# Picking a visit's TensorE work by a time budget in a fused attention and gated-FFN kernel

## The chip, the cores and the metric

The kernel runs on one NeuronCore of a Trainium2 chip. It is one program with five engines: TensorE (PE in the profile; its weight loads are PEld), VectorE (DVE), ScalarE (ACT), GpSimd (POOL) and SyncE (SP). The engines run their own instruction lists in order and meet at semaphores. The metric is the device time of one execution in microseconds.

## The reference

```python
# q, k, v: (8 batches, 8 heads, 1152, 64); w1, w2: (512, 1024); w3: (1024, 1024); w_out: (1024, 512)
q_pool = q.reshape(B, H, S // 2, 2, D).mean(axis=3)          # 576 pooled queries
scores = (q_pool @ k^T) / sqrt(D)
attn   = softmax(scores)
x      = (attn @ v), heads side by side                       # 4608 x 512
h      = ((x @ w1) * (x @ w2)) @ w3
out    = h @ w_out                                            # 4608 x 512, float32
```

The kernel leaves the row maximum out of the softmax (a check at the end of the fast path runs a general path if a row's sum is out of bounds) and multiplies w3 by w_out once, into T, so that the last two products become one.

## The kernel before

**Pairs.** Two heads make a pair; there are 32. For a pair, q's neighbours are added and k and q are cast to 16 bit (kq16, 14 chunks of 128: 9 of k, 4 of q, a tail of q with 64 rows), and transposed into kqT: for pairs 1 to 7 by TensorE (`transp_pe`, L228: fourteen transposes into a psc tile, then three VectorE copies), from pair 8 on by a DMA transpose. GpSimd does the casts (`prepare`, L529, for the pair two ahead) and issues the loads of the first eight pairs and of the weights; SyncE issues the later ones.

**Scores.** A score step s covers 512 of the columns (key chunk by pooled query) of a pair, for both heads: 2 to 4 matmuls into a psc tile of two PSUM banks (there are three psc tiles, used in turn), then one exp on ScalarE into a ring in SBUF (L296). Three steps make a visit (VS = 3), and there are 108 visits.

**AV.** An AV (`av_step`, L558) makes one tile of 128 queries of a pair: 18 small matmuls from the ring and v into the avb bank (L316), then on VectorE a reciprocal and a product, and for the first eight pairs, and every fifth tile, one more transpose of the tile before it by TensorE into the same bank and its copy to xT. Five AVs belong to a pair, and they may start in the visits after the one in which the pair's last score lies.

**Fills.** All other TensorE work is cut into groups that a queue hands out (`fill`, L489). First those of T (`t_groups`, L370): eight transposes of w3 (L379), or eight matmuls of 512 columns that make one row block of T (L388). Then, for each of nine chunks of 512 rows of x, sixteen projections (four matmuls of 512 columns, L409, eight where the rows wrap; VectorE copies the first of a pair, L434, and multiplies the second, L437) and four output groups (eight matmuls, L447, scaled and stored). A group of weight 2 is a row block of T or an output group, the others weigh 1. A fill writes the single mo bank, or, if it is called with `scored`, a psc tile.

**The order.** The loop at L579 writes the instruction lists out: per visit first the three scores, then AVs and fills picked by a running credit: two groups of weight 1 and then an AV, or AV, fill, AV, or a fill of weight 2 and an AV. In a visit with two fills of weight 1 the second one is in psc. After the last visit the remaining AVs alternate with fills, and then the rest of the fills follows with all psc tiles.

**The first pair** has its own code (L241 to L279): its loads are split, the casts of three k chunks and of q are on VectorE and run before the rest, and `first_turn` transposes what is there into the mo bank, with VectorE copying.

Of the kernel before, what the change touches and what calls it, by code (L numbers as in the profile page):

```python
# [8 lines left out]
FP32 = mybir.dt.float32  # L9
# [113 lines left out]
def kernel(  # L123
# [62 lines left out]
    def load_kq(p, k_eng, q_eng):  # L186
        b, h0 = p // HP, 2 * (p % HP)
        kst = att.tile([128, 2, NJ * D], FP32, tag="kst")
        k_eng.dma_start(out=kst, in_=k[b, h0:h0 + 2].rearrange("u (p c) d -> p u (c d)", p=128))
        qst = att.tile([128, 2, QM * 2 * D], FP32, tag="qst")  # L190
        qtl = att.tile([QT, 2, 2 * D], FP32, tag="qtl")
        q_eng.dma_start(out=qst, in_=q[b, h0:h0 + 2, 0:QM * 256].rearrange("u (p c) d -> p u (c d)", p=128))
        q_eng.dma_start(out=qtl, in_=q[b, h0:h0 + 2, QM * 256:S].rearrange("u (p t) d -> p u (t d)", t=2))
        kq[p] = (kst, qst, qtl)

    def load_v(p, eng):
        b, h0 = p // HP, 2 * (p % HP)
# [16 lines left out]
    def cast_v(p):  # L214
        va = vaugs[p % NVA]
        if p < NVA:
            nc.gpsimd.memset(va[:, :, :, D:E1], 1.0 / SCL)
        nc.gpsimd.tensor_copy(out=va[:, :, :, 0:D], in_=vs.pop(p).rearrange("p u (c d) -> p u c d", d=D))  # L218
# [22 lines left out]
    def first_loads():  # L241
        kst = att.tile([128, 2, NJ * D], FP32, tag="kst")
        kv = k[0, 0:2].rearrange("u (p c) d -> p u (c d)", p=128)
        qst = att.tile([128, 2, QM * 2 * D], FP32, tag="qst")
        qtl = att.tile([QT, 2, 2 * D], FP32, tag="qtl")
        qv = q[0, 0:2, 0:QM * 256].rearrange("u (p c) d -> p u (c d)", p=128)
        nc.scalar.dma_start(out=qst[:, 0, :], in_=qv[:, 0, :])
        nc.sync.dma_start(out=kst[:, :, 0:K0 * D], in_=kv[:, :, 0:K0 * D])
        nc.scalar.dma_start(out=qtl, in_=q[0, 0:2, QM * 256:S].rearrange("u (p t) d -> p u (t d)", t=2))
        nc.sync.dma_start(out=qst[:, 1, :], in_=qv[:, 1, :])  # L250
        nc.sync.dma_start(out=kst[:, :, K0 * D:], in_=kv[:, :, K0 * D:])
        kq[0] = (kst, qst, qtl)

    def first_casts():
        kst, qst, qtl = kq.pop(0)
        kv = kst.rearrange("p u (c d) -> p u c d", d=D)
        qv = qst.rearrange("p u (c t d) -> p u c t d", t=2, d=D)
        o = kq16s[0].rearrange("p c u d -> p u c d")
        nc.vector.tensor_copy(out=o[:, :, 0:K0], in_=kv[:, :, 0:K0])
        nc.vector.tensor_tensor(out=o[:, 0, NJ:NJ + QM], in0=qv[:, 0, :, 0], in1=qv[:, 0, :, 1], op=ALU.add)  # L260
        nc.gpsimd.tensor_tensor(out=kq16s[0][0:QT, NJ + QM], in0=qtl[:, :, 0:D], in1=qtl[:, :, D:2 * D], op=ALU.add)
        nc.vector.tensor_tensor(out=o[:, 1, NJ:NJ + QM], in0=qv[:, 1, :, 0], in1=qv[:, 1, :, 1], op=ALU.add)
        nc.gpsimd.tensor_copy(out=o[:, :, K0:NJ], in_=kv[:, :, K0:])
        kqT = att.tile([128, NB, 128], FP16, tag="kqT", bufs=3)
        pairs[0] = (*kq_views(kqT), kqT)

    def first_turn(*parts):
        kq16, kqT = kq16s[0], pairs[0][2]
        pt = ps.tile([128, 512], FP32, tag="mo", bufs=1, name="ptf").bitcast(FP16)
        o = 0  # L270
        for c0, c1 in parts:
            for c in range(c0, c1):
                nc.tensor.transpose(pt[:, o + (c - c0) * 128:o + (c - c0) * 128 + 128],
                                    kq16[:, c].rearrange("p u d -> p (u d)"), ident16)
            o += (c1 - c0) * 128
        o = 0
        for c0, c1 in parts:
            nc.vector.tensor_copy(out=kqT[:, c0:c1].rearrange("p c i -> p (c i)"), in_=pt[:, o:o + (c1 - c0) * 128])
            o += (c1 - c0) * 128  # L279


    def scores(s):
# [87 lines left out]
    def t_groups():  # L370
        w3T = {}

        def turn(ft):
            w3T[ft] = msb.tile([128, NF, 128], FP16, tag="w3T", bufs=2, name="w3T")

            def go(pt):
                ph = pt.bitcast(FP16)
                for a in range(NF):
                    nc.tensor.transpose(ph[:, a * 128:a * 128 + 128],  # L379
                                        w3c[ft // 4][:, ft % 4, a * 128:a * 128 + 128], ident16)  # L380

            return 1, go, lambda pt: nc.vector.tensor_copy(out=w3T[ft].rearrange("p a i -> p (a i)"),
                                                           in_=pt.bitcast(FP16))

        def mult(ft):
            def go(pT):
                for a in range(NF):
                    nc.tensor.matmul(pT, w3T[ft][:, a, :], wosb[:, a, :], start=(a == 0), stop=(a == NF - 1))  # L388

            return 2, go, lambda pT: nc.vector.tensor_copy(out=T16[:, ft, :], in_=pT)  # L390

        yield turn(0)
        for ft in range(NF):
            if ft + 1 < NF:
                yield turn(ft + 1)
            yield mult(ft)

    CH = 512

# [81 lines left out]
    def head():  # L481
        while queue and not ahead:
            try:
                ahead.append(next(queue[0]))
            except StopIteration:
                queue.pop(0)
        return ahead[0][0] if ahead else 0

    def fill(scored=False):  # L489
        n = head()  # L490
        if n:
            _, go, put = ahead.pop()
            pt = bank(scored) if put else None
            go(pt)
            if put:
                put(pt)
        return n
# [4 lines left out]
    def w3_load(r):  # L502
        nc.gpsimd.dma_start(out=w3c[r // 2][:, 2 * (r % 2):2 * (r % 2) + 2, :],
                            in_=moe_w3[256 * r:256 * r + 256, :].rearrange("(c p) f -> p c f", p=128))
# [12 lines left out]
    for t in kq16s:  # L517
        nc.gpsimd.memset(t[QT:128, NB - 1], 0.0)
    first_casts()
    w3_load(0)  # L520
    w_load(wosb, moe_w_out)
    cast_kq(1)
    load_kq(2, nc.gpsimd, nc.gpsimd)
    load_v(1, nc.gpsimd)
    cast_v(0)
    w3_load(1)
    load_kq(3, nc.gpsimd, nc.gpsimd)

    def prepare(p):  # L529
# [44 lines left out]

    NVIS = NS // VS
    seen = -1
    credit = 0.0
    vis = 0
    while vis < NVIS or avn[0] < NU:  # L579
        if vis == T_START:  # L580
            queue.append(t_groups())
        while ready:
            queue.append(moe_groups(ready.pop(0)))
        if vis < NVIS:
            for s in range(vis * VS, vis * VS + VS):
                pn = (s * G + G - 1) // FLAT
                if pn != seen:
                    seen = pn
                    if pn == 0:
                        first_turn((0, K0), (NJ, NB))  # L590
                    if NPE <= pn + 1 < NP:
                        transp(pn + 1)
                    if 0 < pn < NP - 2:
                        prepare(pn + 2)
                    elif pn + 2 == NP:
                        cast_v(NP - 1)
                scores(s)
            if vis == 0:
                first_turn((K0, NJ))
                prepare(2)  # L600
        elif vis > NVIS:
            tail[0] = True
        avail = NT5 * sum(1 for e in pair_end if e < vis) - avn[0]
        turn = [p for p in range(1, NPE) if (p * FLAT // G) // VS - 1 == vis]
        if vis >= NVIS:
            fill(True)
            while avn[0] < NU:
                av_step()
                fill(True)
            break  # L610
        credit = min(credit + NU / (NVIS - 5.0), float(avail)) if avail else 0.0
        two = head() == 2
        n_av = 0 if not avail else 2 if credit >= (2.6 if two else 1.6) and avail > 1 else 1
        credit -= n_av
        n_f = 2 if n_av < 2 else 1
        if n_f == 2 and not turn:
            if not two:
                fill()
            fill(not two)
            if n_av:  # L620
                av_step()
        else:
            if n_av:
                av_step()
            for p in turn:
                transp_pe(p)
            fill()
            if n_av > 1:
                av_step()
        vis += 1  # L630
    tail[0] = True
    x_turn(NU - 1)
# [59 lines left out]
```

## Time and profile before

| | us |
|---|---|
| timed runs (3): median, lowest, highest | 428.07, 425.78, 428.37 |
| profiled execution, its own time | 426.23 |
| its span, first to last instruction | 424.5 |
| busy: TensorE, ScalarE, VectorE, GpSimd | 406.2, 326.0, 201.7, 165.3 |
| exps (L296), 324 of 1.025 mean | 307.9 |
| first exp starts | 7.87 |

All times within the execution count from the first instruction. A row of the timeline gives start, duration, engine, source line, operation, output tile and inputs, shapes, and in brackets how long the engine was idle before it and what ended that. Matmuls are pipelined: the start of a group to the start of the next is what it costs, while its duration also holds the time until its last result is out. The busy share therefore hides short waits.

### The profile page before, as it was taken

What the parts mean: (1) busy time and instruction counts of PE and PEld (TensorE: products, weight loads), DVE (VectorE), ACT (ScalarE), POOL (GpSimd) and SP (SyncE); (2) the same over time, 40 slices, a digit from 0 to 9 for tenths busy, and PEclk for the clock granted to TensorE, in tenths of its full rate; (3) what the DMA queues carried; (4) which work ended last, traced back from release to release, by engine and by line L of the source; (5) the groups of instructions that cost most, each with busy time, mean ns of one, the idle gap of its engine ahead of it and who ended that gap; (6) DMA issues with size and microseconds to landing.
All of it is one profiled execution on the core that took longest, in us unless ns stands there. A gap on an engine that the chain in (4) does not pass through costs nothing.

```text
span 424.5 us, 12640 instructions
## 1 busy us (share of the span) xinstructions
PE 406.2 (96%) x5273; PEld 249.9 (59%) x5273; DVE 201.7 (48%) x592; ACT 326.0 (77%) x358; POOL 165.3 (39%) x205
## 2 busy tenths in 40 slices
PE   4879999999999999999999999999999999999994
PEld 2457666666565656665666656665678756444442
DVE  2245554666355544554455535454355537623240
ACT  3968779889999998999889998999999990223322
POOL 4789966370571526322547314342651011000000
PEclk9999999999999999999999999999999999999998
DMA  8999998988594999969999969999991412020203
GB/s 274 252 306 295 276 301 307 283 217 242 150 284 104 270 280 292 257 131 265 306 182 343 237 155 227 246 299 294 289 203 61 58 63 65 12 101 0 99 2 105
DMA packets 90960, 86.34 MB, mean 203 GB/s; under 512 B 59664, under 2 KB 64272, under 8 KB 90896
## 3 DMA queue, kind: packets, MB, share of 16 engines
q1 hardware_dynamic: 81744, 59.78, 56.7%
q0 software_dynamic: 8720, 25.10, 21.5%
q8 instruction: 42, 0.69, 0.7%
q10 hardware_dynamic: 432, 0.59, 0.5%
q14 instruction: 22, 0.18, 0.2%
HBM read 67.11 MB, written 9.44 MB: 180 GB/s over the span
## 4 chain that ended last, share of the span: by engine, by line
PE 89%; DMA 4%; POOL 2%; DVE 2%; ACT 1%; issue 1%; SPq 0%; ACTq 0%; POOLq 0%
PE avb L316 21%; PE psc L291 18%; PE mot L409 16%; PE mo L409 14%; PE mo L447 10%; PE mot L447 5%; DMA w3c<-in_moe_w_dram 3%; PE mo L388 3%; DMA kst<-in_k_dram 1%; ACT ring L296 1%; PE ptk L233 1%; DVE kqT L235 1%; PE mot L388 0%; PE mol L469 0%; PE avb L349 0%
## 5 line engine op out<-in xcount | busy, mean ns | idle before, releaser
L296 ACT ACTIVATE ring<-psc 128x1024 f16<-128x1024 f32 x324 | 307.9, 1025 | 39.9 <-PE psc L291 38.5
L316 PEld LDWEIGHTS <-ring 128*128 128x128 f16 x2880 | 105.2, 98 | 35.4 <-issue 11.5
L316 PE MATMUL avb<-vaug,ring 128*128 128x65 f16 x2880 | 114.1, 193 | 1.5 <-DVE xT L358 1.5
L291 PE MATMUL psc<-kqT 64*128 64x512 f16 (+7 forms) x1152 | 96.2, 290 | 3.2 <-ACT ring L296 1.3
L205 POOL CAST kq<-kst 128x1152 f16<-128x1152 f32 x31 | 35.7, 1151 | 74.8 <-DMA kqT<-kq 39.2
L291 PEld LDWEIGHTS <-kqT 64*128 64x128 f16 x1152 | 45.7, 95 | 29.3 <-issue 6.1
L334 DVE RECIPROCAL rzall<-avb 128x2 f32<-128x2 f32 x160 | 26.3, 164 | 45.3 <-PE avb L316 29.8
L421 POOL DMA_DIRECT2D out_dram<-osb x21 | 11.7, 555 | 87.2 <-DVE rzall L334 87.2
L409 PEld LDWEIGHTS <-w2sb 128*128 128x128 f16 x320 | 28.3, 97 | 26.8 <-issue 2.9
L409 PEld LDWEIGHTS <-w1sb 128*128 128x128 f16 x320 | 28.0, 97 | 27.1 <-issue 3.5
L447 PEld LDWEIGHTS <-gT 128*128 128x128 f16 x280 | 25.4, 98 | 31.2 <-issue 4.0
L447 PE MATMUL mo<-T,gT 128*128 128x512 f16 x184 | 43.7, 380 | 0.0
L409 PE MATMUL mot<-xT,w2sb 128*128 128x512 f16 (+2 forms) x172 | 41.1, 364 | 0.0
L209 POOL TENSOR_TENSOR kq<-qst 128x512 f16<-128x512 f32 x31 | 39.4, 1272 | 1.1 <-DMA qst<-in_q_dram 1.1
L437 DVE TENSOR_TENSOR gT<-mot,asb 128x512 f16<-128x512 f32 x40 | 27.6, 691 | 23.6 <-PE mot L409 23.6
L218 POOL CAST vaug<-vst 128x1152 f16<-128x1152 f32 x32 | 36.6, 1144 | 5.0 <-DMA vst<-in_v_dram 4.1
L409 PE MATMUL mot<-xT,w1sb 128*128 128x512 f16 (+2 forms) x152 | 38.0, 373 | 0.0
L432 ACT COPY asb<-mot 128x512 f32<-128x512 f32 x20 | 11.7, 587 | 32.7 <-PE mot L409 32.7
L434 DVE COPY asb<-mo 128x512 f32<-128x512 f32 x35 | 24.2, 691 | 25.4 <-PE mo L409 25.4
L409 PE MATMUL mo<-xT,w1sb 128*128 128x512 f16 (+2 forms) x168 | 36.1, 344 | 0.0
L460 DVE TENSOR_SCALAR osb<-mo 128x512 f32<-128x512 f32 x23 | 15.9, 692 | 42.3 <-PE mo L447 42.3
L409 PE MATMUL mo<-xT,w2sb 128*128 128x512 f16 (+2 forms) x148 | 33.0, 351 | 0.0
(67 smaller groups left out, 269.6 us busy)
## 6 DMA issues: line engine op xcount, KB each, us to landing
vst<-in_v_dram SPq DMA_DIRECT2D x25, 576.0 KB, 5.0
kst<-in_k_dram SPq DMA_DIRECT2D x23, 576.0 KB, 5.7
qst<-in_q_dram SPq DMA_DIRECT2D x23, 512.0 KB, 7.2
out_dram<-osb POOLq DMA_DIRECT2D x21, 256.0 KB, 6.1
kst<-in_k_dram POOLq DMA_DIRECT2D x8, 576.0 KB, 10.1
qst<-in_q_dram POOLq DMA_DIRECT2D x8, 512.0 KB, 10.9
vst<-in_v_dram POOLq DMA_DIRECT2D x7, 576.0 KB, 6.9
out_dram<-osb SPq DMA_DIRECT2D x10, 256.0 KB, 2.2
```

Source lines behind the costliest of these rows:

```text
L205: nc.gpsimd.tensor_copy(out=kq16[:, 0:NJ].rearrange("p c u d -> p u c d"), in_=kst.rearrange("p u (c d) -> p u c d", d=D))
L209: eng.tensor_tensor(out=kq16[:, NJ:NJ + QM].rearrange("p c u d -> p u c d"), in0=qv[:, :, :, 0], in1=qv[:, :, :, 1], op=ALU.add)
L218: nc.gpsimd.tensor_copy(out=va[:, :, :, 0:D], in_=vs.pop(p).rearrange("p u (c d) -> p u c d", d=D))
L291: nc.tensor.matmul(psc[:, u, f - s * G:f - s * G + ln], kT2[u * 64:u * 64 + 64, jt, :], qpT[u * 64:u * 64 + 64, i0:i0 + ln], start=True, s ...
L296: nc.scalar.activation(out=ring[:, :, r0:r0 + G], in_=psc, func=AF.Exp, bias=0.0, scale=SCALE)
L316: nc.tensor.matmul(avb[:, o + u * E1:o + u * E1 + E1], ring[:, u, c0:c0 + 128], va[:, u, jt, :], start=(jt == 0 and u == 0), stop=(jt == N ...
L334: nc.vector.reciprocal(out=rzall[:, i, :], in_=av[:, :, D:E1].rearrange("p u o -> p (u o)"))
L409: nc.tensor.matmul(pw[:, d0:d0 + n], wt[:, mc, ft * 128:ft * 128 + 128], xT[:, mc, a:a + n], start=(mc == 0 and d0 == 0), stop=(mc == NC - ...
L434: nc.vector.tensor_copy(out=asb, in_=pa)
L437: nc.vector.tensor_tensor(out=gT[:, ft, :], in0=pb, in1=asb, op=ALU.mult)
L447: nc.tensor.matmul(po, gT[:, ft, tt:tt + 128], T16[:, ft, :], start=(ft == 0), stop=(ft == NF - 1))
L460: nc.vector.tensor_scalar_mul(out=osb, in0=po, scalar1=1.0 / (SCL * SCL))
```

## The change

The change has four parts.

- A visit's work is picked by a budget: 2.35 is added per visit, an AV takes 0.62, a unit of fill weight 0.87, a pair's transposes on TensorE 0.75; work is taken while more than 0.3 is left, and the transposes now come first. Two AVs are never next to each other within the stage while there is a fill, unless many wait.
- T is made two row blocks at a time: two groups of w3 transposes (weight 0.5 each, always both), then four groups of eight 256-column matmuls (weight 1).
- The first pair's transposes go to two PSUM banks at once and its tail to a third place: three k chunks to mo, four q chunks to avb, the tail of q to mo again after the first score. ScalarE copies the k chunks and half of the q chunks, VectorE the other half and the tail. GpSimd casts the three k chunks. The loads of q's second half and of its tail change queues.
- On GpSimd's queue the second w3 load moves ahead of the cast of v for pair 0 and the load of v for pair 1.

```diff
 def first_loads():
-        nc.scalar.dma_start(out=qtl, ...)
-        nc.sync.dma_start(out=qst[:, 1, :], in_=qv[:, 1, :])
+        nc.scalar.dma_start(out=qst[:, 1, :], in_=qv[:, 1, :])
+        nc.sync.dma_start(out=qtl, ...)
 def first_casts():
-        nc.vector.tensor_copy(out=o[:, :, 0:K0], in_=kv[:, :, 0:K0])
-        nc.vector.tensor_tensor(out=o[:, 0, NJ:NJ + QM], ...)
+        nc.gpsimd.tensor_copy(out=o[:, :, 0:K0], in_=kv[:, :, 0:K0])
+        for u in range(2):
+            nc.vector.tensor_tensor(out=o[:, u, NJ:NJ + QM], ...)
         nc.gpsimd.tensor_tensor(out=kq16s[0][0:QT, NJ + QM], ...)
-        nc.vector.tensor_tensor(out=o[:, 1, NJ:NJ + QM], ...)
-        nc.gpsimd.tensor_copy(out=o[:, :, K0:NJ], in_=kv[:, :, K0:])
+    def rest_casts():
+        nc.gpsimd.tensor_copy(..., in_=kv[:, :, K0:])
-    def first_turn(*parts):
+    def first_turn(c0, c1, pt, *engs):
+        for c in range(c0, c1):
+            nc.tensor.transpose(pt[:, (c - c0) * 128:(c - c0) * 128 + 128], ...)
+        w = (c1 - c0) // len(engs)
+        for n, eng in enumerate(engs):
+            o = n * w
+            eng(out=kqT[:, c0 + o:c0 + o + w]..., in_=pt[:, o * 128:(o + w) * 128])
...
-            return 1, go, lambda pt: nc.vector.tensor_copy(out=w3T[ft]...)
+            return 0.5, go, lambda pt: nc.vector.tensor_copy(out=w3T[ft]...)
-        def mult(ft):
+        def mult(ft, n0):
             def go(pT):
                 for a in range(NF):
-                    nc.tensor.matmul(pT, w3T[ft][:, a, :], wosb[:, a, :], ...)
-            return 2, go, lambda pT: nc.vector.tensor_copy(out=T16[:, ft, :], in_=pT)
+                    nc.tensor.matmul(pT[:, 0:256], w3T[ft][:, a, :], wosb[:, a, n0:n0 + 256], ...)
+            return 1, go, lambda pT: nc.vector.tensor_copy(out=T16[:, ft, n0:n0 + 256], in_=pT[:, 0:256])
-        yield turn(0)
-        for ft in range(NF):
-            if ft + 1 < NF:
-                yield turn(ft + 1)
-            yield mult(ft)
+        for ft in range(0, NF, 2):
+            yield turn(ft)
+            yield turn(ft + 1)
+            for n in range(4):
+                yield mult(ft + n // 2, n % 2 * 256)
...
     load_kq(2, nc.gpsimd, nc.gpsimd)
+    w3_load(1)
+    cast_v(0)
     load_v(1, nc.gpsimd)
-    cast_v(0)
-    w3_load(1)
...
-                        first_turn((0, K0), (NJ, NB))
+                        first_turn(0, K0, turn_bank(), nc.scalar.copy)
+                        first_turn(NJ, NJ + QM, avb.bitcast(FP16), nc.vector.tensor_copy, nc.scalar.copy)
                 scores(s)
+                if s == 0:
+                    first_turn(NB - 1, NB, turn_bank(), nc.vector.tensor_copy)
...
-        credit = min(credit + NU / (NVIS - 5.0), float(avail)) if avail else 0.0
-        two = head() == 2
-        n_av = 0 if not avail else 2 if credit >= (2.6 if two else 1.6) and avail > 1 else 1
...
+        budget += 2.35
+        for p in turn:
+            transp_pe(p)
+            budget -= 0.75
+        n_av = n_f = 0
+        if avail > 3:
+            was_av = False
+        while True:
+            late = avail > 3 and n_av < 2
+            if avail and (budget > 0.3 or late) and not (was_av and head()):
+                av_step()
+                avail -= 1
+                n_av += 1
+                budget -= 0.62
+                was_av = True
+            elif head() and budget > 0.3:
+                two_turns = head() < 1
+                budget -= 0.87 * fill(n_f == 1)
+                n_f += 1
+                if two_turns and head() < 1:
+                    budget -= 0.87 * fill(n_f == 1)
+                    n_f += 1
+                was_av = False
+            else:
+                budget = min(budget, 0.0)
+                break
```

More of the change, by code (lines that the diff above doesn't have):

```diff
@@ L248, in first_loads @@
         nc.sync.dma_start(out=kst[:, :, 0:K0 * D], in_=kv[:, :, 0:K0 * D])
-        nc.scalar.dma_start(out=qtl, in_=q[0, 0:2, QM * 256:S].rearrange("u (p t) d -> p u (t d)", t=2))
-        nc.sync.dma_start(out=qst[:, 1, :], in_=qv[:, 1, :])
+        nc.scalar.dma_start(out=qst[:, 1, :], in_=qv[:, 1, :])
+        nc.sync.dma_start(out=qtl, in_=q[0, 0:2, QM * 256:S].rearrange("u (p t) d -> p u (t d)", t=2))
         nc.sync.dma_start(out=kst[:, :, K0 * D:], in_=kv[:, :, K0 * D:])
@@ L254, in first_casts @@
     def first_casts():
-        kst, qst, qtl = kq.pop(0)
+        kst, qst, qtl = kq[0]
         kv = kst.rearrange("p u (c d) -> p u c d", d=D)
@@ L258, in first_casts, with turn_bank @@
         o = kq16s[0].rearrange("p c u d -> p u c d")
-        nc.vector.tensor_copy(out=o[:, :, 0:K0], in_=kv[:, :, 0:K0])
-        nc.vector.tensor_tensor(out=o[:, 0, NJ:NJ + QM], in0=qv[:, 0, :, 0], in1=qv[:, 0, :, 1], op=ALU.add)
+        nc.gpsimd.tensor_copy(out=o[:, :, 0:K0], in_=kv[:, :, 0:K0])
+        for u in range(2):
+            nc.vector.tensor_tensor(out=o[:, u, NJ:NJ + QM], in0=qv[:, u, :, 0], in1=qv[:, u, :, 1], op=ALU.add)
         nc.gpsimd.tensor_tensor(out=kq16s[0][0:QT, NJ + QM], in0=qtl[:, :, 0:D], in1=qtl[:, :, D:2 * D], op=ALU.add)
-        nc.vector.tensor_tensor(out=o[:, 1, NJ:NJ + QM], in0=qv[:, 1, :, 0], in1=qv[:, 1, :, 1], op=ALU.add)
-        nc.gpsimd.tensor_copy(out=o[:, :, K0:NJ], in_=kv[:, :, K0:])
         kqT = att.tile([128, NB, 128], FP16, tag="kqT", bufs=3)
         pairs[0] = (*kq_views(kqT), kqT)
-    def first_turn(*parts):
+    def rest_casts():
+        kv = kq.pop(0)[0].rearrange("p u (c d) -> p u c d", d=D)
+        nc.gpsimd.tensor_copy(out=kq16s[0].rearrange("p c u d -> p u c d")[:, :, K0:NJ], in_=kv[:, :, K0:])
+    def first_turn(c0, c1, pt, *engs):
         kq16, kqT = kq16s[0], pairs[0][2]
[L269 to L279, printed above, removed]
+        for c in range(c0, c1):
+            nc.tensor.transpose(pt[:, (c - c0) * 128:(c - c0) * 128 + 128],
+                                kq16[:, c].rearrange("p u d -> p (u d)"), ident16)
+        w = (c1 - c0) // len(engs)
+        for n, eng in enumerate(engs):
+            o = n * w
+            eng(out=kqT[:, c0 + o:c0 + o + w].rearrange("p c i -> p (c i)"), in_=pt[:, o * 128:(o + w) * 128])
+    def turn_bank():
+        return ps.tile([128, 512], FP32, tag="mo", bufs=1, name="ptf").bitcast(FP16)
     def scores(s):
@@ L380, in go @@
                                         w3c[ft // 4][:, ft % 4, a * 128:a * 128 + 128], ident16)
-            return 1, go, lambda pt: nc.vector.tensor_copy(out=w3T[ft].rearrange("p a i -> p (a i)"),
+            return 0.5, go, lambda pt: nc.vector.tensor_copy(out=w3T[ft].rearrange("p a i -> p (a i)"),
                                                            in_=pt.bitcast(FP16))
-        def mult(ft):
+        def mult(ft, n0):
             def go(pT):
                 for a in range(NF):
-                    nc.tensor.matmul(pT, w3T[ft][:, a, :], wosb[:, a, :], start=(a == 0), stop=(a == NF - 1))
-            return 2, go, lambda pT: nc.vector.tensor_copy(out=T16[:, ft, :], in_=pT)
-        yield turn(0)
-        for ft in range(NF):
-            if ft + 1 < NF:
-                yield turn(ft + 1)
-            yield mult(ft)
+                    nc.tensor.matmul(pT[:, 0:256], w3T[ft][:, a, :], wosb[:, a, n0:n0 + 256],
+                                     start=(a == 0), stop=(a == NF - 1))
+            return 1, go, lambda pT: nc.vector.tensor_copy(out=T16[:, ft, n0:n0 + 256], in_=pT[:, 0:256])
[4 more added lines that the diff above has]
+                yield mult(ft + n // 2, n % 2 * 256)
     CH = 512
@@ L519 @@
     first_casts()
+    rest_casts()
     w3_load(0)
@@ L576 @@
     seen = -1
-    credit = 0.0
+    budget = -0.6
+    was_av = False
     vis = 0
@@ L597 @@
                 scores(s)
+                if s == 0:
+                    first_turn(NB - 1, NB, turn_bank(), nc.vector.tensor_copy)
             if vis == 0:
-                first_turn((K0, NJ))
+                first_turn(K0, NJ, turn_bank(), nc.vector.tensor_copy)
                 prepare(2)
@@ L610 @@
             break
-        credit = min(credit + NU / (NVIS - 5.0), float(avail)) if avail else 0.0
-        two = head() == 2
-        n_av = 0 if not avail else 2 if credit >= (2.6 if two else 1.6) and avail > 1 else 1
[L614 to L620, printed above, removed]
-                av_step()
[L622 to L629, printed above, removed]
+        budget += 2.35
[8 more added lines that the diff above has]
+            if avail and (budget > 0.3 or late) and not (was_av and head()):
+                av_step()
+                avail -= 1
[9 more added lines that the diff above has]
+                    n_f += 1
+                was_av = False
+            else:
+                budget = min(budget, 0.0)
+                break
         vis += 1
```

## The prediction

> **What bounds the kernel now.** I read the page first: engine shares, slices, chain.
>
> ```profile
> PE 406.2 (96%) x5273; PEld 249.9 (59%) x5273; DVE 201.7 (48%) x592; ACT 326.0 (77%) x358; POOL 165.3 (39%) x205
> ...
> PE 89%; DMA 4%; POOL 2%; DVE 2%; ACT 1%; issue 1%; SPq 0%; ACTq 0%; POOLq 0%
> ```
>
> TensorE is busy 96% of the span and is 89% of the chain that ended last. An average over stages says little, so the busy sums by stretch come next (span 424.5 us, cut at 29, 75 and 345 us).
>
> ```profile
> core 0: us, PE busy (x) PEld busy (x) DVE busy (x) ACT busy (x) POOL busy (x), PEclk, DMA share, GB/s
> 0.00:29.00 29.00, 18.64 (x196) 11.35 (x198) 8.35 (x21) 18.28 (x19) 19.95 (x34) 1.00 1.01 275
> 29.00:75.00 46.00, 44.12 (x689) 29.73 (x689) 24.05 (x87) 39.10 (x42) 36.56 (x49) 1.00 1.01 297
> 75.00:345.00 270.00, 269.56 (x3896) 172.15 (x3896) 138.32 (x417) 246.06 (x259) 106.04 (x119) 1.00 0.92 223
> 345.00:424.50 79.50, 73.91 (x503) 36.63 (x497) 31.02 (x70) 22.58 (x39) 2.73 (x5) 0.98 0.18 58
> ```
>
> From 75 us on TensorE never stops (269.56 of 270), while ScalarE is idle 24 us. All TensorE work is fixed in amount, so from there a new order can only add stalls or remove what is hardly there. Something can be won in the first 29 us (10.4 us idle) and in 29:75 (1.9 us idle, and some more hidden in stretched matmuls).
>
> Then the timeline, for what a stall looks like. Columns: start, duration, engine, line, operation; the bracket is idle time and who ended it.
>
> ```profile
> 17.99 0.95 PE L379 MATMUL mo<-ident,w3c 128*128 128x128 f16 x8
> ...
> 18.78 0.61 PE L379 MATMUL mot<-ident,w3c 128*128 128x128 f16 x8
> ...
> 19.32 0.74 PE L291 MATMUL psc<-kqT 64*128 64x192 f16 x8
> ...
> 19.58 0.68 DVE L382 COPY w3T<-mot 128x1024 f16<-128x1024 f16 x1
> ...
> 20.32 0.39 PE L291 MATMUL psc<-kqT 64*128 64x320 f16 x4 [0.26 <-DVE w3T L382]
> ```
>
> This is visit 3, the only visit of the scores' stage (108 in all) that ends in a fill that borrowed a psc bank. There are three psc tiles, used in turn: three scores, then the fill takes the first again, so the next visit's **third** score is the one that must wait until VectorE has emptied the fill's. It started 1.00 us after its visit (20.32 − 19.32); in an undisturbed visit the third score starts at 0.447 (median from 75 us on, by the starts of single matmuls).
>
> ```profile
> 127.34 0.94 PE L291 MATMUL psc<-kqT 64*128 64x512 f16 x10
> ...
> 129.09 1.03 PE L409 MATMUL mot<-xT,w1sb 128*128 128x512 f16 x4
> ...
> 129.95 0.71 PE L316 MATMUL avb<-vaug,ring 128*128 128x65 f16 x18
> ...
> 130.15 0.69 DVE L434 COPY asb<-mot 128x512 f32<-128x512 f32 x1 [0.17 <-PE mot L409]
> ...
> 130.59 0.61 PE L291 MATMUL psc<-kqT 64*128 64x192 f16 x8
> ```
>
> Here the same borrowing costs nothing: an AV of 0.6 us follows the fill, and VectorE is done at 130.84, before the third score at 130.59 + 0.447 = 131.04. So the tile is free 0.89 us after the fill's successor begins, plus 0.05 (20.27 to 20.32) for the signal.
>
> **The change, part by part.**
>
> *The picks (visits 4 to 107).* Following the loop's arithmetic: 2.35 a visit, 0.62 for an AV, 0.87 for a unit of fill. Two AVs and a projection (2.11) leave 0.24, below 0.3; a projection, an AV and a projection (2.36) are the other usual visit. As two AVs may not touch, the second kind is always fill, AV, fill, and the last fill is in psc (its number is 1). 23 visits end that way (20, 23, 26, 29, 36, ... 106); before, this order was fill, fill, AV. The scores now follow the fill directly. Price of one: the fill's last matmul starts 0.216 before an AV could; the tile is free 0.216 + 0.89 + 0.05 = 1.16 after that matmul; without the wait the third score would come at 0.216 + 0.447 = 0.66. That is **0.50 lost**, in it about 0.09 for scores behind 512-column matmuls (T at 61.41 to the scores at 63.23: 1.82, elsewhere 1.73). 23 × 0.50 = 11.5 us. Ends: 0.35 (no such 0.09, VectorE 0.06 earlier) and 0.60 (the 0.55 of visit 3 and some queue on VectorE), 8.1 to 13.8. The AV behind the third score, and all after it, waits in TensorE's one order; ScalarE, with its 24 us idle, is not held up.
>
> The other boundaries: 16 more visits end in a fill in mo, 16 × 0.09 = 1.4, against 38 fewer scores behind an AV at 0.05 (AV before scores 0.607, before a fill 0.554), 1.9: near zero together, counted as zero. 15 more visits begin with an AV, where the scores' block takes 0.785 instead of 0.758: 0.4.
>
> *Transposes of q and k on TensorE (pairs 2 to 7) move to the front of their visit*, right behind the scores. They take a psc tile too, that of the visit's first score, and so wait for its exp:
>
> ```profile
> 14.44 1.65 PE L233 MATMUL ptk<-ident,kq 128*128 128x128 f16 x14 [0.31 <-ACT ring L296]
> ...
> 66.51 0.83 PE L291 MATMUL psc<-kqT 64*128 64x384 f16 x10
> ...
> 67.00 2.85 ACT L296 ACTIVATE ring<-psc 128x1024 f16<-128x1024 f32 x3 [0.42 <-PE psc L291]
> ...
> 68.77 0.71 PE L316 MATMUL avb<-vaug,ring 128*128 128x65 f16 x18 [0.72 <-DVE xT L358]
> ```
>
> The first line is pair 1, which stood so already. Later an exp begins 0.49 after its scores and takes 1.02: free at 1.51, 1.57 with the signal, against 0.77 when the scores are issued. 0.80 for each of pairs 3 to 7 (pair 2 is in the opening below) is 4.0 us; ends 0.31 (the row shown) and 0.85: 1.5 to 4.3. Before, an AV stood between, and at 50.68 the fourteen took 0.78 with no wait.
>
> *Removed.* The last line above: AV 19 directly behind AV 18 waits for VectorE; its boundary costs 0.93 where 0.05 is usual. That was the only such pair before. Three lone w3 transposes between AVs (33.54, 45.91, 57.34) took 0.88, 0.81, 0.88 instead of 0.45; T waited twice 0.17 for its copy (42.72, 53.53), pair transposes twice 0.18, a third score once 0.32 (58.91). Together 0.88 + 1.23 + 0.34 + 0.36 + 0.32 = 3.1 us, all gone if the new order has none of its own; ends 1.5 and 3.6.
>
> *T in halves.* Sixteen groups of eight 256-column matmuls (16 such take 1.76 us at L469, so 0.88 each), 14.1 us, for eight of 1.73, 13.8: 0.2 us. VectorE's copies of half size are hidden, but two halves in a row in visit 3 share mo.
>
> *The opening.* q's second half lands at 4.91 and its add ends at 5.35, as before. But four transposes (5.41 on) no longer wait for q's tail (6.09), and VectorE and ScalarE copy side by side: scores at about 6.5 instead of 7.22, first exp at 7.15 instead of 7.87. GpSimd's cast of k (0.36 on VectorE, some 0.5 by its 0.82 for twice the size) ends near 4.6, long before. The tail's add ends at 6.0, its transposition stands behind score 0, its copy is there at 7.5, and score 1 is in time for the exp at 8.15. ScalarE then runs without a break to visit 3, 0.7 early.
>
> Visit 3 takes T0 into its own: w3 transposes to 18.6, then T0 waits for wosb, which landed at 20.11 and whose place in GpSimd's queue is the same. First half 20.15 to 21.05, copied by 21.65; second half to 22.6, as it reuses mo. Scores of visit 4 at 22.6 (19.32 before), AV 0, half of T1, AV 1, scores of visit 5 at 25.55 to 26.35 (a tile waits for an exp at 26.0), pair 2 at 27.05 (its exp; GpSimd's casts end at 25.06), half of T1, AV 2, scores of visit 6 at 29.4. Before, that point was 28.96, but with one w3 transposition (0.45) more and T1 (1.73) less done: 0.8 us won. The second w3 load, now ahead of v's, lands some 2 us earlier than 27.76, so the 1.73 us wait for it goes; late next are the exp and mo. v of pair 1 lands 2 us later, and behind its cast stand on GpSimd the loads for pairs 2 and 4, and pair 3's casts, done near 35 and needed near 39. Ends: 2.0 won (wosb earlier) and 1.7 lost.
>
> Until 18.7 TensorE issued a w3 transpose every 0.108 us, then every 0.056 (the lines at 17.99 and 18.78: 0.95 and 0.61); the record of the granted clock begins there. Should it go on at the slower pace through T0 and the scores of visit 4, that is 2 × 0.88 + 0.76 = 2.5 us more; I count on the same turning point, as what it has to do before 18.7 is the same.
>
> The Trainium skill, "TensorE: Matmul & The Clock Gate", Part 1, says that TensorE runs at half rate until some 3.4 us of sustained work and falls back after such an idle window. The pace at 17.99 agrees; that the new wait for wosb would trip it, no row shows. By that rule the sum could be 441.
>
> **Sum.** 11.5 + 4.0 + 0.4 + 0.2 − 3.1 − 0.8 = +12.2. The profiled execution took 426.23 (span 424.5): 438.4. The three timed runs have 425.78 to 428.37, median 428.07, 1.8 above it; I say **438.5**. Ends added up: 8.1 + 1.5 + 0.6 − 3.6 − 2.0 = +4.6 and 13.8 + 4.3 + 0.6 − 1.5 + 1.7 = +18.9, so 431 to 445.
>
> **The rivals.**
>
> *Faster, at 420.* The opening gives all that its rows lose (0.7 of the start, 1.73 for w3, 0.56 of pair 2's wait at 25.12, 0.5 of visit 4's scores: 3.5), 29:75 its 3.1, and psc never binds: 426.2 − 6.6 + 0.6. For it: TensorE's 10.4 idle us. Against it: the tile that visit 3 waited for. It decides at 6.0 us of psc waits: with 4.0 for pairs 3 to 7, at 0.09 for each of the 23 visits. Chance 0.10.
>
> *The picks change little, 427.* The sum of work is the same, and at 127.34 (third score 0.10 late, waiting for the exp that held its tile) ScalarE's pace already costs a visit what a full tile would. Then 23 × 0.10 + 1.5 − 3.9 + 0.6 = +0.5. Against it: VectorE's copy alone takes 0.69. Chance 0.10.
>
> *Above 443.* The slower pace goes on (2.5 us), and the dear ends of the fills' and the transposes' terms come with it: 438.4 + 2.5 + 2.3 + 0.3 = 443.5. Chance 0.07.
>
> *The forecast,* 431 to 443, as the dear ends will not all come together: 0.73.
>
> A change of 1% (4.3 us) is about what timing can tell from none. Faster 0.10, same 0.10, slower 0.80. The range takes in the upper half of the second rival too (0.07 with what lies up to 431): 427 to 443.
>
> **What would show it.** Right: third scores that wait for VectorE's gT or asb copies, in 23 visits, blocks of scores of 1.25 to 1.3 us there; pairs 2 to 7 waiting for ring; TensorE's idle share up to some 6%; first exp near 7.2. Wrong: scores' blocks of 0.85 behind a fill, or scores that reach visit 6 before 28 us with T1 done.

## The result, and the profile after

The changed kernel is slower. Six runs lie between 436.62 and 441.1 us with a median of 437.33; the kernel before has 426.0 (424.73 to 428.37). The ratio is 1.0284, with a 95% interval of 1.0255 to 1.0314. The profiled execution took 440.21 us and spans 438.3.

The page of the changed kernel, engine shares and chain by engine:

```profile
PE 412.3 (94%) x5337; PEld 253.0 (58%) x5337; DVE 202.5 (46%) x596; ACT 328.4 (75%) x363; POOL 165.6 (38%) x206
...
PE 81%; DMA 6%; ACT 6%; DVE 4%; issue 2%; POOL 0%; SPq 0%; ACTq 0%; DVEq 0%
```

TensorE fell from 89% to 81% of the chain; ScalarE (1% before) and VectorE (2%) now hold 6% and 4% of it: somewhere TensorE waits for them in turn. The busy sums by stretch, with the columns as in the prediction (the stretch, its length, then PE, PEld, DVE, ACT and POOL busy, TensorE's granted clock, DMA share, GB/s), say where:

```profile
0.00:29.00 29.00, 20.21 (x165) 12.61 (x167) 6.48 (x17) 16.49 (x18) 18.11 (x32) 1.00 0.99 275
29.00:75.00 46.00, 42.83 (x751) 34.39 (x746) 25.95 (x94) 39.28 (x42) 38.76 (x51) 1.00 0.99 283
75.00:345.00 270.00, 261.69 (x3759) 159.31 (x3755) 133.19 (x404) 240.11 (x254) 106.03 (x119) 1.00 0.92 224
345.00:438.30 93.30, 87.61 (x675) 46.67 (x672) 36.87 (x83) 32.52 (x51) 2.73 (x5) 0.99 0.16 51
```

From 75 to 345 us TensorE did 269.56 us before; now 261.69, and 137 matmuls fewer. The waits of the changed kernel (who waited, for whom: us in all, times, longest) name three kinds:

```profile
PE ptk L233 <- ACT ring L298: 4.6, 7, 0.7
...
PE psc L293 <- DVE gT L440: 3.7, 16, 0.2
...
PE psc L293 <- DVE asb L437: 1.6, 7, 0.2
```

16 and 7 are 23: the 23 visits that end in a fill in a psc tile. Each is counted as 0.2 us only, because a matmul's modelled end runs into the wait; the timeline from start to start gives the whole price. One such place:

```profile
81.45 1.02 PE L412 MATMUL mot<-xT,w2sb 128*128 128x512 f16 x4
...
82.41 0.61 PE L293 MATMUL psc<-kqT 64*128 64x512 f16 x6
82.52 0.69 DVE L440 TENSOR_TENSOR gT<-mot,asb 128x512 f16<-128x512 f32 x1 [0.23 <-PE mot L412]
82.91 1.94 ACT L298 ACTIVATE ring<-psc 128x1024 f16<-128x1024 f32 x2 [0.34 <-PE psc L293]
83.26 0.39 PE L293 MATMUL psc<-kqT 64*128 64x128 f16 x4 [0.24 <-DVE gT L440]
83.59 0.72 PE L318 MATMUL avb<-vaug,ring 128*128 128x65 f16 x18
```

VectorE empties the fill's tile from 82.52 to 83.21, and the third score starts at 83.26. The scores' block is 1.18 us long (82.41 to 83.59); behind a fill in mo it is 0.76. All 23 blocks are 1.17 or 1.18.

The transpositions behind the scores:

```profile
75.31 0.83 PE L293 MATMUL psc<-kqT 64*128 64x192 f16 x12
...
76.88 0.94 PE L233 MATMUL ptk<-ident,kq 128*128 128x128 f16 x14 [0.74 <-ACT ring L298]
```

From the scores to them it is 1.57 us, where 0.76 is enough: 0.81 lost, in each of five visits.

### The profile page after: what moved, and what is told of

Same layout as the page of the kernel before. It is cut to its first block, busy times and chain, and to the rows that moved or that the text cites. A ratio compares the mean times of both kernels' runs of the same rounds, so it can differ in the third digit from the quotient of the medians.

```text
span 438.3 us, 12771 instructions
## 1 busy us (share of the span) xinstructions
PE 412.3 (94%) x5337; PEld 253.0 (58%) x5337; DVE 202.5 (46%) x596; ACT 328.4 (75%) x363; POOL 165.6 (38%) x206
## 4 chain that ended last, share of the span: by engine, by line
PE 81%; DMA 6%; ACT 6%; DVE 4%; issue 2%; POOL 0%; SPq 0%; ACTq 0%; DVEq 0%
PE avb L318 20%; PE psc L293 15%; PE mot L412 14%; PE mo L412 13%; PE mo L450 7%; PE mot L450 6%; ACT ring L298 5%; PE mo L390 3%; DMA wosb<-in_moe_w_out_dram 3%; DVE gT L440 3%; DMA xT<-xb 2%; PE ptk L233 1%; DMA kst<-in_k_dram 1%; DVE asb L437 1%; PE mol L472 0%
## 5 line engine op out<-in xcount | busy, mean ns | idle before, releaser
L318 PEld LDWEIGHTS <-ring 128*128 128x128 f16 x2880 | 103.9, 98 | 32.2 <-issue 11.4
L293 PE MATMUL psc<-kqT 64*128 64x512 f16 (+7 forms) x1152 | 100.6, 292 | 9.8 <-DVE gT L440 3.7
L412 PE MATMUL mot<-xT,w2sb 128*128 128x512 f16 (+2 forms) x180 | 42.1, 360 | 0.0
L412 PE MATMUL mo<-xT,w1sb 128*128 128x512 f16 (+1 forms) x192 | 41.3, 344 | 0.0
L437 DVE COPY asb<-mo 128x512 f32<-128x512 f32 x40 | 27.7, 692 | 28.6 <-PE mo L412 28.6
L435 ACT COPY asb<-mot 128x512 f32<-128x512 f32 x23 | 13.5, 585 | 36.2 <-PE mot L412 36.2
L450 PE MATMUL mo<-T,gT 128*128 128x512 f16 x160 | 37.8, 379 | 0.0
L412 PE MATMUL mot<-xT,w1sb 128*128 128x512 f16 x128 | 32.8, 379 | 0.0
L412 PE MATMUL mo<-xT,w2sb 128*128 128x512 f16 (+2 forms) x140 | 31.9, 355 | 0.0
L344 DVE TENSOR_TENSOR xb<-avb,rzall 128x128 f16<-128x128 f32 x96 | 28.0, 292 | 3.5 <-DMA xT<-xb 0.3
```

What stands on the lines that cost most here:

```text
L293: nc.tensor.matmul(psc[:, u, f - s * G:f - s * G + ln], kT2[u * 64:u * 64 + 64, jt, :], qpT[u * 64:u * 64 + 64, i0:i0 + ln], start=True, s ...
L318: nc.tensor.matmul(avb[:, o + u * E1:o + u * E1 + E1], ring[:, u, c0:c0 + 128], va[:, u, jt, :], start=(jt == 0 and u == 0), stop=(jt == N ...
L344: nc.vector.tensor_tensor(out=xbt, in0=av[:, :, 0:D], in1=rzall[:, i, :].unsqueeze(2).to_broadcast([128, 2, D]), op=ALU.mult)
L412: nc.tensor.matmul(pw[:, d0:d0 + n], wt[:, mc, ft * 128:ft * 128 + 128], xT[:, mc, a:a + n], start=(mc == 0 and d0 == 0), stop=(mc == NC - ...
L437: nc.vector.tensor_copy(out=asb, in_=pa)
L450: nc.tensor.matmul(po, gT[:, ft, tt:tt + 128], T16[:, ft, :], start=(ft == 0), stop=(ft == NF - 1))
```

## The experiments

Theory A says that the loss is psc tiles that are wanted before they are empty: a visit's last fill makes the next third score wait for VectorE, and leading transpositions wait for an exp. Theory B says that the budget makes visits uneven, so that ScalarE's pace of three exps (2.85 us) sets the time of some.

The experiments ran on three chips, with medians of 426.22, 426.03 and 425.86 for the kernel before, so a difference between kernels that ran on different chips holds to some tenths.

**The transpositions moved behind the first group of their visit.**

```diff
-        budget += 2.35
-        for p in turn:
-            transp_pe(p)
-            budget -= 0.75
+        budget += 2.35 - 0.75 * len(turn)
...
         while True:
+            if n_av + n_f:
+                while turn:
+                    transp_pe(turn.pop(0))
...
+        while turn:
+            transp_pe(turn.pop(0))
```

> The changed kernel with one thing altered: the six q and k transpositions on TensorE (pairs 2 to 7) come after the first group picked in their visit instead of straight behind the scores; the picks stay the same. Theory A (a transposition behind the scores waits for the exp that holds its psc tile, 0.81 us each): about 6 x 0.75 = 4.5 us less than the changed kernel, 433, and scores' blocks of 0.76 to 0.79 in those visits. Theory B (the loss comes from uneven visits that the budget makes, and ScalarE's pace): no difference, 437. Scores behind psc fills stay at 1.18.

Measured: 434.65 us (434.03 to 435.29), 1.0194 of the kernel before (1.0166 to 1.0222). That is 2.7 under the changed kernel where 4.5 was expected. That is against Theory B; Theory A has the direction, and the trace shows what it left out:

```profile
82.22 0.94 PE L233 MATMUL ptk<-ident,kq 128*128 128x128 f16 x14
...
83.00 0.71 PE L318 MATMUL avb<-vaug,ring 128*128 128x65 f16 x18
83.20 1.22 DVE L235 COPY kqT<-ptk 128x768 f16<-128x768 f16 x3
83.55 0.22 PE L351 MATMUL avb<-ident,xbt 128*128 128x128 f16 x1
83.70 1.17 PE L293 MATMUL psc<-kqT 64*128 64x384 f16 x10
```

The wait for ring is gone, but the transpositions hold a psc tile too, and its three copies end at 84.42: the third score, due at 83.70 + 0.447 = 84.15, is 0.3 late. The five scores' blocks that follow transpositions and an AV are 1.10 to 1.12 us long from start to start instead of 0.78: some 0.32 each, 1.6 us of the 1.8 that are missing. The kernel before had another fill in between.

**The order fill, fill, AV instead of fill, AV, fill.**

```diff
             if avail and (budget > 0.3 or late) and not (was_av and head()):
+                both = n_f == 1 and n_av == 0 and head() == 1 and budget - 0.62 > 0.3 and avail <= 4
+                if both:
+                    budget -= 0.87 * fill(True)
+                    n_f += 1
                 av_step()
...
-                was_av = True
+                was_av = not both
```

> The changed kernel with 21 of its 23 visits of the order fill, AV, fill turned to fill, fill, AV; the same groups in every visit. Theory A (the third score of the next visit waits until VectorE has emptied the last fill's psc tile, 0.49 us each, against 0.08 for scores behind an AV): 21 x 0.42 = 8.8 us less than the changed kernel, about 428.5, and blocks of 0.76 to 0.90 where 1.18 stood. Theory B (uneven visits, ScalarE's pace): the visits hold the same work, so 437.

Measured: 429.62 us (429.46 to 430.02), 1.008 (1.0054 to 1.0106): 7.7 less than the changed kernel, for 21 visits with the same work in each. Theory B is out for these 21. A visit's end in the repaired kernel:

```profile
78.63 0.59 PE L412 MATMUL mot<-xT,w2sb 128*128 128x512 f16 x2
...
79.06 0.71 PE L318 MATMUL avb<-vaug,ring 128*128 128x65 f16 x18
79.26 0.69 DVE L440 TENSOR_TENSOR gT<-mot,asb 128x512 f16<-128x512 f32 x1 [0.17 <-PE mot L412]
...
79.76 0.83 PE L293 MATMUL psc<-kqT 64*128 64x512 f16 x10
```

VectorE's 0.69 us now lies beside the AV. The waits of the scores for gT are no longer in the list, and of the seven for asb two are left (0.4 us), with the two blocks of 1.18 behind the two visits that were not turned.

**Both repairs.** The two diffs above, together.

> Both of these alterations of the changed kernel together. Theory A: the savings add up, 13.3 us, to 424, a little below the kernel before (426). Theory B: 437. If the two waits cover each other (a late third score hides the late transposition), clearly less than the sum, 428 or more.

Measured: 427.01 us (12 runs, 426.33 to 427.7) beside 426.22; ratio 1.0014 (0.9998 to 1.0030). The savings of the two alone, 2.7 and 7.7, add up to the 10.3 found. So undoing the two orders takes the loss away: the rest of the change (T, opening, budget) makes no difference in sum that these runs can tell. That is a balance. The blocks behind the transpositions still lose 1.7 us here and the two of 1.18 another 0.8, and the w3 load with the grouping of T wins 2.5, under the picks of the kernel before, by a run below.

**The same order put into the kernel before.**

```diff
...
             if not two:
                 fill()
+            if n_av and not two and head() == 1:
+                av_step()
+                n_av = 0
             fill(not two)
             if n_av:
                 av_step()
```

> The kernel before, with one thing altered: in its 29 visits with two fills of weight 1 and an AV, the AV stands between the fills instead of behind them; nothing else of the change. Theory A: 29 x 0.42 = 12 us more than the kernel before, 438, with scores' blocks of 1.18. Theory B: the visits hold the same work, so 426.

Measured: 435.82 us (435.59 to 437.27), 1.0231 (1.0202 to 1.0261): 9.6 us lost by this edit alone, for 29 visits.

```profile
98.74 1.02 PE L409 MATMUL mot<-xT,w1sb 128*128 128x512 f16 x4
...
99.70 0.61 PE L291 MATMUL psc<-kqT 64*128 64x512 f16 x6
99.80 0.69 DVE L434 COPY asb<-mot 128x512 f32<-128x512 f32 x1 [0.24 <-PE mot L409]
...
100.54 0.40 PE L291 MATMUL psc<-kqT 64*128 64x128 f16 x4 [0.24 <-DVE asb L434]
100.87 0.72 PE L316 MATMUL avb<-vaug,ring 128*128 128x65 f16 x18
```

The picture is the same, and all 29 blocks are 1.17 or 1.18 long. That it is 0.33 a visit and not 0.42 fits what the kernel before showed at 127.34: there third scores were often 0.1 late already, for an exp, and much of that lateness is now inside the longer wait. Added up from visit 6 on, what the other blocks last beyond 0.77 each falls from 4.0 us in the kernel before to 2.4 here.

**VectorE empties the second fill's tile twice.**

```diff
...
             if put:
                 put(pt)
+                if twice and scored:
+                    put(pt)
...
-                budget -= 0.87 * fill(n_f == 1)
+                budget -= 0.87 * fill(n_f == 1, True)
...
```

> The changed kernel, in which VectorE empties the psc tile of a visit's second fill twice (the same copy or product once more, 0.69 us each); VectorE is busy 46% of the span. Theory A (VectorE's copy is what the third score waits for): 23 visits x 0.69 = 16 us more, some 453, scores' blocks of 1.87 there. If the 0.42 comes from something else (weights that load late behind a fill, an exp): VectorE has room, 437.

Measured: 454.74 us (454.71 to 455.65), 16.9 above the changed kernel beside it (437.79). The 23 blocks grew from 1.18 to 1.89: 0.72 each, 16.5 in all.

```profile
91.70 0.61 PE L293 MATMUL psc<-kqT 64*128 64x512 f16 x6
91.81 1.42 DVE L440 TENSOR_TENSOR gT<-mot,asb 128x512 f16<-128x512 f32 x2 [0.24 <-PE mot L412]
92.20 2.86 ACT L298 ACTIVATE ring<-psc 128x1024 f16<-128x1024 f32 x3 [0.34 <-PE psc L293]
93.27 0.40 PE L293 MATMUL psc<-kqT 64*128 64x128 f16 x4 [0.96 <-ACT ring L298]
```

An engine that is busy 46% of the span passes 0.69 us of extra work on in full at these places. The bracket names ScalarE here, though the pair of products ends at 93.23 and sets the start: the exp that began at 92.20 (1.02) ends 0.01 before it. In the changed kernel the third score of the same kind of visit started at 83.26, with the exp that began at 82.91 still running, so it does not wait for that exp. The times have to be read, not the name.

**The changed kernel once more.** The same code, so there is no diff.

> The changed kernel once more, beside the others on one chip: 437. In the profiled execution of it TensorE went to its full rate at 27.1 us only and the time was 440.2; in the others, where w3's transposes, T and the first scores of visit 4 take the full rate from about 20 us, some 3 us less is expected. Theory: whether it is 437 or 440 hangs on where that turn falls, not on the order of the work.

Measured: 437.79 us (437.71 to 437.88). In this profile the record of the full TensorE clock begins at 21.6 us and the span is 435.8; in the first one it begins at 27.1 and the span is 438.3. The rows of the first:

```profile
18.24 1.03 PE L381 MATMUL mo<-ident,w3c 128*128 128x128 f16 x8
...
19.06 1.06 PE L381 MATMUL mot<-ident,w3c 128*128 128x128 f16 x8
...
20.47 1.86 PE L390 MATMUL mo<-wosb,w3T 128*128 128x256 f16 x8 [0.34 <-DMA wosb<-in_moe_w_out_dram]
...
22.85 1.86 PE L390 MATMUL mo<-wosb,w3T 128*128 128x256 f16 x8 [0.52 <-DVE T L393]
```

And the two halves of T0 in the second:

```profile
20.58 1.54 PE L390 MATMUL mo<-wosb,w3T 128*128 128x256 f16 x8
...
22.64 1.03 PE L390 MATMUL mo<-wosb,w3T 128*128 128x256 f16 x8 [0.52 <-DVE T L393]
```

From visit 3 to visit 6 it took 16.2 us (16.27 to 32.51), against 13.6 (16.80 to 30.36) in the second profile. What decides where the turn falls was not tried and stays open: the two traces have the same code and the same order.

**The opening alone, in the kernel before.** `first_loads`, `first_casts`, `rest_casts`, `first_turn` and their calls as in the change's diff; nothing else.

> The kernel before with the first pair's part of the change alone (two banks at once, its tail after the first score, ScalarE's copies, GpSimd's cast of k, the two loads exchanged); picks, T and the w3 load as before. The prediction's opening step: first exp 0.7 us earlier and kept, 425.5. What the changed kernel's trace suggests instead: the first exp 0.4 earlier, but the tail's transposition and copy stand between the first two scores and the rest of k lands 0.35 later, so that the fourth exp is no earlier: 426.2, no difference.

Measured: 427.21 us (425.49 to 429.12, 12 runs) beside 426.03; ratio 1.002 (0.9996 to 1.0044). No difference, as the second reading expected and the prediction did not.

```profile
6.48 0.29 DVE L278 COPY kqT<-avb 128x256 f16<-128x256 f16 x1 [0.70 <-PE avb L273]
...
6.80 0.37 ACT L278 COPY kqT<-avb 128x256 f16<-128x256 f16 x1 [0.83 <-DVE kqT L278]
...
7.88 3.08 ACT L298 ACTIVATE ring<-psc 128x1024 f16<-128x1024 f32 x3 [0.70 <-PE psc L293]
...
8.38 1.04 PE L293 MATMUL psc<-kqT 64*128 64x64 f16 x8 [0.32 <-DVE kqT L278]
...
11.31 1.94 ACT L298 ACTIVATE ring<-psc 128x1024 f16<-128x1024 f32 x2 [0.35 <-PE psc L293]
```

ScalarE's half of the copy does not run beside VectorE's; it waits for it. Both read the avb bank; that this is the reason was not tried. Score 1 waits for the tail's copy, so that the second exp starts 1.15 after the first, where the kernel before had 0.92, and the rest of k is transposed later, so that the fourth exp waits 0.35 more. It comes 3.43 after the first; before it was 2.73 (7.87 to 10.60).

The start of the first exp differs between executions of one opening by half a microsecond, so a single pair of profiles misleads. Over all profiles it is at 7.43 to 7.95 with the new opening (seven) and at 7.87 to 8.40 with the old one (five), and the fourth exp at 10.87 to 11.39 and at 10.60 to 11.13. By the means the new opening is 0.36 earlier at the first exp and 0.35 later at the fourth.

**A mix.** The kernel with both repairs, with the opening of the kernel before, and with AV, transpositions, fill, AV in the visits of pairs 2 to 7 where the next fill has weight 1, which is five of the six:

```diff
...
+        if turn and avail > 1 and head() == 1:
+            av_step()
+            transp_pe(turn.pop(0))
+            fill()
+            av_step()
+            budget -= 0.62 * 2 + 0.87
+            avail -= 2
+            n_av, n_f = 2, 1
+            was_av = True
...
```

> The kernel with both repairs (fill, fill, AV; transpositions not behind the scores), and further with the opening of the kernel before, and with the order AV, transpositions, fill, AV in the visits of pairs 2 to 7; T by pairs, the early w3 load and the budget stay. Theory A: the last stall of the repaired kernel, 0.3 us for the third score behind transpositions in five visits, goes: 425.5, level with the kernel before. If the new opening had been worth something, 427 or more.

Measured: 431.87 us (431.18 to 433.11), 1.0137 (1.0106 to 1.0168): a miss, 6 us above what was expected. The four picks overdraw the budget (2.86 taken of 2.35), and this shifts all picks after them. Ten visits now end in psc again, four of these with an output group of 1.73; others are left with one projection:

```profile
118.24 1.04 PE L410 MATMUL mo<-xT,w1sb 128*128 128x512 f16 x4
119.21 0.39 PE L291 MATMUL psc<-kqT 64*128 64x512 f16 x2
119.96 0.39 PE L291 MATMUL psc<-kqT 64*128 64x64 f16 x4 [0.36 <-ACT ring L296]
120.88 0.40 PE L291 MATMUL psc<-kqT 64*128 64x128 f16 x4 [0.52 <-ACT ring L296]
```

A visit of 1.5 us (117.71 to 119.21) is far shorter than its three exps, and TensorE waits for ScalarE: 2.0 us for a scores' block. This is Theory B's mechanism. It exists, and where visits are this light it costs more than a late tile. The blocks tell where most of the 4.9 us against the repaired kernel lie. From visit 6 on, beyond 0.77 each, those behind psc fills are 3.9 us longer in all, 1.8 are saved behind the transpositions, and the other blocks are 2.3 longer.

**The second w3 load alone.** In the kernel before, the load moved as in the change's last lines on GpSimd's queue.

> The kernel before with the second w3 load moved ahead of the cast of v for pair 0 and the load of v for pair 1, nothing else. The prediction's step: the wait of 1.73 us for w3 at 26 us goes, and what is late next is pair 2's transposition (ready at 25.1): 424.5, TensorE's third w3 transposition at 26.1 instead of 27.8. Rival: the wait only moves, as v of pair 1 is cast later and the loads behind it are issued later: 426.

Measured: 424.45 us (423.64 to 425.67, 12 runs) beside 425.86; ratio 0.9963 (0.9945 to 0.9980). The step counts, and what is late next is close behind:

```profile
25.23 0.95 PE L233 MATMUL ptk<-ident,kq 128*128 128x128 f16 x14
...
26.78 0.62 PE L379 MATMUL mo<-ident,w3c 128*128 128x128 f16 x8 [0.60 <-DMA w3c<-in_moe_w_dram]
...
28.26 1.15 POOL L218 CAST vaug<-vst 128x1152 f16<-128x1152 f32 x1 [2.97 <-DMA vst<-in_v_dram]
```

The wait for w3 is 0.60 instead of 1.73. The cast of v for pair 1 is indeed later (25.47 before), and nobody waited for it.

**T by pairs and in halves, with that load.** In the kernel before, `t_groups` as in the change (weight 1 for each turn) and the load moved; credit, picks and opening as before.

> The kernel before with T by pairs of w3 transpositions and halves of 256 columns, and with the same move of the w3 load; the picks, by credit, and the opening stay those of the kernel before. Prediction's steps: besides the w3 wait, the waits behind lone w3 transpositions (three of four go, 0.9), the adjacent AVs (0.9) and T's waits for its copy (0.3) go, and the halves cost 0.2: 422.5. Against it: two visits of two w3 transpositions and an AV (2.3 us of work) are shorter than three exps (2.85), 0.5 each: 423.5. If nothing of it counts: 426.

Measured: 423.37 us (422.45 to 426.01, 11 runs) beside 425.86; ratio 0.9938 (0.9919 to 0.9958). This is the best kernel found, under 1% faster than the kernel before. 2.5 us are won, 1.4 of them by the load alone, and the value lies by the expectation that counts the light visits (423.5). Those two are in the trace; behind each, the scores' block is 1.26 long, as in this one (33.37 to 34.63):

```profile
33.37 0.39 PE L291 MATMUL psc<-kqT 64*128 64x384 f16 x4
...
34.09 0.61 PE L291 MATMUL psc<-kqT 64*128 64x448 f16 x6 [0.32 <-ACT ring L296]
...
34.63 0.72 PE L316 MATMUL avb<-vaug,ring 128*128 128x65 f16 x18
```

## Why the prediction was right, point by point

The sum said +12.2 on a profiled execution of 426.23; the profiled pair differs by 14.0, and the medians by 11.3. Its terms:

- **Third scores behind a psc fill, 23 × 0.50 = 11.5.** The mechanism is shown, the net size is smaller. There are 23 waits in the list; the block is 1.18 instead of 0.785 behind an AV, and 0.095 goes to the boundary behind a fill, 0.49 together. (The prediction's sign of blocks of 1.25 to 1.3 had that boundary in the block a second time.) Undoing it gave 7.7 for 21, adding it cost 9.6 for 29, doubling VectorE's part cost 16.9. In the net it is 0.33 to 0.37 a visit, some 8 us for 23, because the AV in front of the scores has a boundary of its own and the old order already paid some lateness to the exps. The prediction weighed the first against the fills in mo and left the second out. It took the AV's boundary as 0.05; the starts give 0.08 to 0.09 (an AV takes 0.644 before scores, 0.560 before a projection).
- **Transpositions, 5 × 0.80 = 4.0.** Shown: 0.81 in each of the five visits. It is not what one gets back by moving them one place, since they hold their tile for 1.22 us of copies.
- **Removed in the stage of T, −3.1.** Right, and a little too large. Start to start, the adjacent AVs (0.88), the waits in front of pair transpositions (0.69, in four places where the prediction counted two) and those behind lone w3 transpositions (1.23, of which 0.65 stay) fell by 2.2; the waits of T for its copy (0.34) and the one late third score (0.32) are gone too, 2.8 in all. By the runs, T by pairs won 1.1 under the old picks, which have two light visits with it.
- **The opening, −0.8.** This gain did not come. Its first step, "VectorE and ScalarE copy side by side", failed: ScalarE waited for VectorE (6.36 after 6.03 in the changed kernel), and the first exp came at 7.43, not 7.15. Its second, "ScalarE then runs without a break", failed too: the fourth exp came at 10.87, where before it was 10.60. Alone, the opening is worth nothing that the runs can tell.
- **Visits 3 to 6.** The w3 wait went, as forecast (1.4 us by its own run). T0 waited for mo in both profiles (0.52), for wosb only in the first (0.34). Scores of visits 4, 5 and 6 were forecast at 22.6, 25.55 and 29.4; the second profile has 23.61, 26.50 and 30.36, all about a microsecond late. Its T0 began at 20.58 where 20.15 was forecast, and the first half of it, partly before the turn, took 0.5 longer than the second (1.54 and 1.03). In the first profile the slower pace went on to 27.1 us, the case that the prediction priced at 2.5 and held unlikely; visits 3 to 6 took 2.7 longer than in the second. That the prediction's "same turning point" does not hold is shown by the records: they begin at 18.7 in the kernel before, at 27.1 and 21.6 in the changed one, at 19.9 to 21.6 in the others.

Taken together in the profiled pair: up to visit 6 the changed kernel is at 32.51 against 28.96, with 1.28 us more work done, so 2.3 lost where 0.8 was to be won. After it, 405.8 us against 395.5 and the 1.28 less to do: 11.6 lost where 13.0 were forecast. In the second profile, whose time (437.83) is near the median, it is 0.1 and 11.2. Each time the two errors, 3.1 and 1.4 or 0.9 and 1.8, have opposite signs. The mechanism was right, but that the sum is closer than its parts is luck.

The Trainium skill, "TensorE: Matmul & The Clock Gate", Part 1, has the array at half rate until it has been busy long enough. The trace agrees in the two paces: a transposition every 0.107 us before the turn and every 0.056 after it. It does not account for when the turn comes here: by the Trainium skill some 3.4 us of sustained work are enough, while in the first profile TensorE was busy for 11.2 of the 12.4 us from 14.69 to 27.1, with no wait over 0.52. The prediction's 2.5 us for a late turn, worked out from its rows, stand beside 2.5 between the two profiled spans.

The rivals: that the fills' waits do not bind is out by the list of 23; that ScalarE's pace levels the orders is out for the changed kernel by the repaired orders, though the mix shows the mechanism at work. ScalarE's pace costs something in both kernels: from visit 6 on, the blocks that stand neither behind a psc fill nor in front of transpositions last 4.4 us in all beyond 0.77 each in the changed kernel (five, behind light visits, are 1.13 to 1.45 long), and 4.0 in the kernel before, 0.7 of these the waits of T's stage that went. So it makes about 1 us of the difference.

## What to carry to other kernels

Where one engine is always busy, count for every reordering which buffer of a rotating set the next user takes, and put the longest other work between a buffer's last write and that user; the same two fills and one AV cost 0.33 to 0.37 us more here with the AV in the middle. A budget of one engine's time does not see this, nor that a visit must last as long as the other engine's part. Parts of a change are worth trying singly: of this one, an earlier load and the grouping of T are gains, while the two orders cost more than all of it.

## What the runs showed of the hardware

TensorE's turn to full rate in the opening falls at 18.7 to 21.6 us in eleven profiles and at 27.1 in one, whose code turned at 21.6 another time; the spans of these two differ by 2.5 us.

The idle time that the profile gives for a wait in front of matmuls was well under what the wait cost: 5.3 us for the 23 late scores, whose blocks are 0.40 longer from start to start, 9.1 in all.
